# First layer of a top-1 expert network in arms of 256 and 320 columns, and rank matmuls ordered behind transposes

## The chip, the cores and the metric

One core of one Trainium2 chip runs the kernel. The metric is the device time of one execution in microseconds; times before are the median of three runs. PE is TensorE, DVE is VectorE, ACT is ScalarE, POOL is GpSimd and SP is SyncE, which issues most transfers.

## The reference

Two steps. The first is a kind of attention between 512 tokens and 32 state rows in each of 8 batches and 8 heads (head size 64), in both directions. Its output has 544 rows for each batch and 512 columns (all heads side by side), 4352 rows in all. The second sends each row to one of 8 experts, the one with the largest logit, and runs that expert's two layers on it:

```python
scores = scale * x @ state.T          # per batch and head; softmax over state
xread = a @ state
scores2 = scale * state @ x.T         # softmax over tokens
sread = a2 @ x
x = concat([xread, sread])            # (4352, 512)
logits = x @ w_gate; e_idx = argmax(logits, axis=1)
for e in range(8):
    mask = e_idx == e
    h = maximum(x[mask] @ w1[e], 0.0)          # 512 -> 1024
    ye = h @ w2[e]                             # 1024 -> 512
    out[mask] = gate_w[mask, None] * eom[mask, e, None] * ye
```

Matrix products are held to float32 quality: a factor is split into a high and a low part, and a product takes three matmuls (high by high, high by low, low by high).

## The kernel before

**Attention stage.** Batches follow each other in a software pipeline; a scheduler sets the order of instructions on each engine from their dependences, so that the order of PE is not the order of the source. For each batch PE transposes x (`x_trans`, L325), transposes the softmax of the other direction (`e2_trans`, L419), computes scores (L337), transposes the row softmax (`a_trans`, L359) and the scores for the softmax over columns (`columns_softmax`, L401), reads states (`state_reads`, L431) and reads tokens (`token_reads`, L380 to L382). After four batches the state rows get their logits (`state_out`, L444). When a group of batches has its logits, `route` (L221) finds each token's expert (the one-hot `ohb`), its rank among its expert's tokens, by matmuls with a triangle and with ones (L243 to L247), and its place in a table, by one matmul for each tile of 128 tokens into `tid_ps` (L300). PSUM has three double buffers `psb` for this stage and one buffer `pss`, which ranks and state reads share.

**Routing tables.** From the counts of each expert DVE works out tiles of 128 tokens, and from those units: two tiles a unit, an odd last tile joins its expert's last unit as a third, and an expert with a single tile has a unit of one (L507 to L581). `route_i` holds for each unit its size, whether it begins an expert, and which expert's weights to load next. Engines read these into registers and branch on them.

**Expert stage.** Written in order by hand (`manual_schedule`). For each unit `first` (L641) computes the first layer for all of the unit's tokens at once, 8 blocks of 12 matmuls, in an arm with 384 columns for three tiles and one with 256 columns otherwise; ACT and DVE turn each block into `hhi` and `hlo`. Then `second` (L666) runs 24 matmuls of 512 columns for one tile. Tile 0 is always run, tile 1 if the size is at least 2, tile 2 if it is 3. The other side of each of these branches is `nothing` (L660), one tiny matmul and a copy. Between them PE transposes the next unit's tokens (`x_transposed`, L611), two tiles and a third one if that unit has it. POOL gathers the tokens of the unit after next and scatters results by index. Where a unit begins an expert, ACT and DVE split the new weights into `whi` and `wlo`. First-layer results use four PSUM buffers `p1`, second-layer results two buffers `po`.

Of the kernel before, what the change touches and what calls it, by code (L numbers as in the profile page):

```python
# [9 lines left out]
F32 = mybir.dt.float32  # L10
# [4 lines left out]
ALU = mybir.AluOpType  # L15
# [6 lines left out]
def attention_then_top1_experts(ctx: ExitStack, tc: tile.TileContext, x, state, w_gate, w_og, w1, w2, out):  # L22
# [9 lines left out]
    W = 3  # L32
    NU = (NT - E + 1) // 2 + E
    NX = NU + NT // 2
# [6 lines left out]
    NQ = NT * E  # L41
    SURE = (NT - E) // 2

# [39 lines left out]
    unit_f = const.tile([1, NU], F32, name="unit_f")  # L83
    nc.gpsimd.tensor_copy(unit_f, un_i)

    def after(inst, before):
# [32 lines left out]
    with ExitStack() as actx:  # L119
# [101 lines left out]
        def route(lgs, nch, tile0, write):  # L221
# [67 lines left out]
            for c0 in range(0, nch, 3):  # L289
# [105 lines left out]
        def columns_softmax(b):  # L395
# [28 lines left out]
        def state_reads(b):  # L424

            xb, e2T = xbs[b], st["e2T", b]
            sr = pss.tile([P, 512], F32, name="pss", tag="pss")
            srv = sr.rearrange("p (h k n) -> p h k n", h=H, k=2)
            for h in range(H):
                for cc in range(2):  # L430
                    nc.tensor.matmul(srv[:, h], lhsT=xb[:, h, 2 * cc : 2 * cc + 2, :].rearrange("p c d -> p (c d)"),  # L431
                                     rhs=e2T[:, 2 * cc : 2 * cc + 2, NS * h : NS * h + NS], start=(cc == 0), stop=(cc == 1))
# [98 lines left out]
        r1 = slice(0, 1)  # L531
        nc.vector.scalar_tensor_tensor(ODD[r1], in0=LONE[r1], scalar=-2.0, in1=ODD[r1], op0=ALU.mult, op1=ALU.add)
        nc.vector.tensor_scalar(LAST[r1], SUM[r1], 1.0, None, op0=ALU.subtract)
# [57 lines left out]
    KH = DF // P  # L591
    NTOKU = W * P

    xg_all = [[bp1.tile([P, ROWW], F32, name=f"xg{u}{i}") for i in range(W)] for u in range(3)]
    xT_all = [[bp1.tile([P, KX, NTOKU], F32R, name=f"x{n}{u}") for n in ("hi", "lo")] for u in range(2)]
    hhi = bp1.tile([P, KH, NTOKU], F32R, name="hhi")
    hlo = bp1.tile([P, KH, NTOKU], F32R, name="hlo")
    rest_of = bp1.tile([P, 8], F32, name="rest_of")
# [12 lines left out]
    def x_transposed(u, i):  # L611
# [5 lines left out]
        for k in range(KX):  # L617
            nc.tensor.transpose(tp[:, k, :], xg_all[u % 3][i][:, P * k : P * k + P], ident)  # L618
        c = slice(P * i, P * i + P)
        nc.scalar.copy(hi[:, :, c], tp)  # L620
        nc.vector.tensor_sub(lo[:, :, c], tp, hi[:, :, c].bitcast(F32))  # L621

# [18 lines left out]
    def first(u, n, chg):  # L641

        hi, lo = xT_all[u % 2]
        for fb in range(KH):
# [7 lines left out]
            if fb in (0, 3):  # L652
                upper(2 if fb == 0 else 3, chg)
            nc.scalar.activation(hhi[:, fb, :n], p1[:, :n], AF.Relu)  # L654
            nc.vector.scalar_tensor_tensor(hlo[:, fb, :n], in0=p1[:, :n], scalar=0.0, in1=hhi[:, fb, :n].bitcast(F32),  # L655
                                           op0=ALU.max, op1=ALU.subtract)
            if fb in (1, 4):
# [8 lines left out]
    def second(u, t, between=None):  # L666
        po = py.tile([P, DM], F32, name="po", tag="po")
        c = slice(P * t, P * t + P)
        for j in (2, 3):
# [6 lines left out]
            for k in range(4):  # L676
# [5 lines left out]
                                     in_=y, in_offset=None)  # L682

    def values(u):
        if u >= NU:
            return None
        size = nc.values_load(route_i[0:1, 0, u : u + 1], engines=[ET.PE, ET.Activation, ET.DVE, ET.Pool], min_val=0, max_val=3,
                              skip_runtime_bounds_check_because="2, with one more for an odd number's last tile, or one less for an only one")
        if u == 0:
# [7 lines left out]
    def unit(u):  # L697
        size, chg, nxt = val[u]
        with tc.If(size == 3) as odd:
            first(u, NTOKU, chg)  # L700
        with odd.Else():
            first(u, 2 * P, chg)
# [11 lines left out]
        if more:  # L714
            x_transposed(u + 1, 1)
            with tc.If(more[0] == 3) as three:  # L716
                x_transposed(u + 1, 2)
            with three.Else():
# [5 lines left out]
        with tc.If(size == 3) as three:  # L724
            second(u, 2)
        with three.Else():
            nothing(py, "po")
# [46 lines left out]
```

## Time and profile before

| what | value |
|---|---|
| median of three runs (lowest, highest) | 660.9 us (660.82, 661.13) |
| the profiled execution, its time | 661.41 us |
| its span, first to last instruction | 659.7 us |
| PE busy | 615.5 us (93%) |
| VectorE, ScalarE, GpSimd busy | 283.4, 245.3, 176.9 us |
| mean granted clock of TensorE | 0.968 |

[...] Busy shares are means over two stages with different limits: the attention stage up to about 188 us, and the expert stage after it. Starts are in microseconds from the first instruction; a matmul's shown duration includes its way through the array, so that the time between starts, not the duration, says how fast matmuls follow each other.

### The profile page before, as it was taken

The page shows a single profiled execution, that of the slowest core. Times are in us where ns is not written, and L with a number is a line of the kernel's source. Part 1 is how long each engine was busy: PE and PEld are TensorE (multiplying, and loading weights), DVE is VectorE, ACT ScalarE, POOL GpSimd, SP SyncE. Part 2 cuts the span into 40 slices and gives each one's busy share as a digit, 9 for nine tenths or more (in the row PEclk, how much of TensorE's full clock was granted, in tenths as well). Part 3 has the DMA queues.
Part 4 walks back from the last instruction along what each step waited for, and adds up shares of the span by engine and source line. Part 5 has one row for each costly group of instructions (what it writes and reads, how often), then busy time and mean ns, then how long its engine had stood idle before and what let it go on. Part 6 is the DMA issues. An engine that isn't in the chain of part 4 may idle for free. (4 is left out here: it accounts for less than half of the span.)

```text
span 659.7 us, 11415 instructions
## 1 busy us (share of the span) xinstructions
PE 615.5 (93%) x3941; PEld 552.3 (84%) x3941; DVE 283.4 (43%) x622; ACT 245.3 (37%) x411; POOL 176.9 (27%) x254
## 2 busy tenths in 40 slices
PE   7899898998689999999999999999999999999990
PEld 5898797897468998998989989899898998988980
DVE  5547858979863211221235243144132514463210
ACT  3566536556042222222334244244233324472210
POOL 8135505531042221121122203123112220322210
PEclk8999979999779999999999999999999999999996
DMA  8534432322265220220145225326315523475210
GB/s 224 212 128 131 141 119 80 129 69 98 53 229 194 68 82 19 67 83 33 51 161 194 82 83 173 125 80 233 117 52 173 182 82 105 154 249 188 67 35 19
DMA packets 46289, 78.57 MB, mean 119 GB/s; under 512 B 11056, under 2 KB 19248, under 8 KB 46192
## 3 DMA queue, kind: packets, MB, share of 16 engines
q1 hardware_dynamic: 38592, 52.00, 23.9%
q0 software_dynamic: 7600, 25.38, 11.4%
q8 instruction: 49, 0.80, 0.5%
q14 instruction: 48, 0.39, 0.2%
HBM read 101.98 MB, written 19.42 MB: 184 GB/s over the span
## 5 line engine op out<-in xcount | busy, mean ns | idle before, releaser
L655 DVE SCALAR_TENSOR_TENSOR hlo<-p,hhi 128x256 fp32r<-128x256 f32 (+1 forms) x136 | 62.0, 462 | 224.8 <-ACT hhi L654 212.0
L648 PE MATMUL p<-xhi,whi 128*128 128x256 f32 (+1 forms) x544 | 151.0, 300 | 0.9 <-ACT rest_of L664 0.5
L649 PE MATMUL p<-xhi,wlo 128*128 128x256 f32 (+1 forms) x544 | 149.8, 298 | 0.0
L681 POOL DMA_INDIRECT out_dram<-y,idx x38 | 39.4, 1038 | 316.0 <-ACT y L680 228.0
L674 PE MATMUL po<-whi,hhi 128*128 128x512 f32 x304 | 122.6, 403 | 0.0
L675 PE MATMUL po<-wlo,hhi 128*128 128x512 f32 x304 | 120.1, 395 | 0.0
L654 ACT ACTIVATE hhi<-p 128x256 fp32r<-128x256 f32 (+1 forms) x136 | 56.2, 415 | 135.7 <-PE p L651 132.8
L648 PEld LDWEIGHTS p<-xhi,whi 128*128 128x128 f32 x544 | 103.4, 190 | 2.1 <-ACT rest_of L664 1.2
L649 PEld LDWEIGHTS p<-xhi,wlo 128*128 128x128 f32 x544 | 103.3, 190 | 0.3 <-issue 0.2
L651 PE MATMUL p<-xlo,whi 128*128 128x256 f32 (+1 forms) x544 | 95.8, 298 | 0.0
L678 PE MATMUL po<-whi,hlo 128*128 128x512 f32 x304 | 83.2, 395 | 0.0
L607 POOL DMA_INDIRECT xg<-xa,idx x57 | 68.4, 1200 | 49.5 <-issue 16.2
L651 PEld LDWEIGHTS p<-xlo,whi 128*128 128x128 f32 x544 | 81.1, 190 | 0.0
L680 ACT ACTIVATE y<-po,xg 128x512 f32<-128x512 f32 x38 | 26.1, 688 | 132.5 <-issue 49.1
L678 PEld LDWEIGHTS po<-whi,hlo 128*128 128x128 f32 x304 | 57.0, 187 | 14.0
L675 PEld LDWEIGHTS po<-wlo,hhi 128*128 128x128 f32 x304 | 57.2, 188 | 11.6
L674 PEld LDWEIGHTS po<-whi,hhi 128*128 128x128 f32 x304 | 57.1, 188 | 11.5
L635 DVE TENSOR_TENSOR wlo<-stage,whi 128x2048 fp32r<-128x2048 f32 x24 | 54.4, 2286 | 11.6 <-ACT whi L628 11.6
L621 DVE TENSOR_TENSOR xlo<-pxT,xhi 128x512 fp32r<-128x512 f32 x39 | 25.9, 687 | 62.4 <-ACT xhi L620 62.4
L628 ACT CAST whi<-stage 128x2048 fp32r<-128x2048 f32 x24 | 45.1, 1902 | 3.9 <-DVE hlo L655 1.7
L620 ACT CAST xhi<-pxT 128x512 fp32r<-128x512 f32 x39 | 22.2, 583 | 30.7 <-PE pxT L618 30.7
L337 PE MATMUL psb<-sT,xT 128*128 128x64 f32 x256 | 32.7, 289 | 0.2 <-ACT xT L327 0.2
(189 smaller groups left out, 728.2 us busy)
## 6 DMA issues: line engine op xcount, KB each, us to landing
stage<-in_moe_w_dram SPq DMA_DIRECT2D x74, 1024.0 KB
xb<-in_x_dram SPq DMA_DIRECT2D x7, 1024.0 KB
xa<-xm SPq DMA_DIRECT2D x7, 1024.0 KB
xb<-in_x_dram SPq DMA_DIRECT2D x2, 512.0 KB
xa<-xm SPq DMA_DIRECT2D x4, 256.0 KB
xg<-xa,idx POOLq DMA_INDIRECT x57, 3.6
out_dram<-y,idx POOLq DMA_INDIRECT x38, 3.1
sraw<-in_state_dram SPq DMA_DIRECT2D x2, 256.0 KB
```

Source lines behind the costliest of these rows:

```text
L607: g = nc.gpsimd.indirect_dma_start(out=xg_all[u % 3][i], out_offset=None, in_=xa[:, :], in_offset=bass.IndirectOffsetOnAxis(ap=ix, axis=0))
L628: nc.scalar.copy(whi[i], stage[i])
L635: nc.vector.tensor_sub(wlo[i], stage[i], whi[i].bitcast(F32))
L648: nc.tensor.matmul(p1[:, :n], lhsT=whi[i][:, k, c], rhs=hi[:, k, :n], start=(k == 0), stop=False)
L649: nc.tensor.matmul(p1[:, :n], lhsT=wlo[i][:, k, c], rhs=hi[:, k, :n], start=False, stop=False)
L651: nc.tensor.matmul(p1[:, :n], lhsT=whi[i][:, k, c], rhs=lo[:, k, :n], start=False, stop=(k == KX - 1))
L654: nc.scalar.activation(hhi[:, fb, :n], p1[:, :n], AF.Relu)
L655: nc.vector.scalar_tensor_tensor(hlo[:, fb, :n], in0=p1[:, :n], scalar=0.0, in1=hhi[:, fb, :n].bitcast(F32), op0=ALU.max, op1=ALU.subtract)
L674: nc.tensor.matmul(po, lhsT=hhi[:, f, c], rhs=whi[j][:, k, :], start=(f == 0), stop=False)
L675: nc.tensor.matmul(po, lhsT=hhi[:, f, c], rhs=wlo[j][:, k, :], start=False, stop=False)
L678: nc.tensor.matmul(po, lhsT=hlo[:, f, c], rhs=whi[j][:, k, :], start=False, stop=(f == KH - 1))
L681: nc.gpsimd.indirect_dma_start(out=out[:, :], out_offset=bass.IndirectOffsetOnAxis(ap=idx[:, W * u + t : W * u + t + 1], axis=0), in_=y, i ...
```

## The change

Three things are changed. The third tile joins a unit only if it holds at most 64 tokens; the first layer then has 256 + 64 = 320 columns, and the third tile's 64 tokens lie with their high and low parts side by side in one stationary operand of 128 (`hfew`), so that its second layer (`second_few`) takes 16 matmuls and the two halves of the result are added afterwards. An odd tile with more tokens gets a unit of its own of size 1. Sizes are now 1, 2 and 4, the tables hold 24 units instead of 21, and 14 units instead of 13 run without asking whether they exist. In the attention stage an order without a wait is asked for: a group's first rank matmul and its matmuls into `tid_ps` stand on PE behind the last column transposes or state reads that were written before them, except near the end of the stage.

```diff
-    NU = (NT - E + 1) // 2 + E
+    NU = NT // 2 + E - 1
-    SURE = (NT - E) // 2
+    HP = P // 2
+    FEW = 2 * P + HP
+    SURE = -(-NTOK // FEW)
...
+    def behind(inst, before):
+        tc.add_manual_dep(inst.ins, before.ins.name, mybir.DependencyInfo(mybir.DependencyClass.NoSync, mybir.DependencyReason.DATA), reason="order")
...
-            nc.tensor.matmul(rkv, lhsT=tri, rhs=ohb, start=True, stop=False)
+            m = nc.tensor.matmul(rkv, lhsT=tri, rhs=ohb, start=True, stop=False)
+            if len(done) < NT - 5:
+                behind(m, st["pe"])
...
                     done.append(nc.tensor.matmul(tid_ps, lhsT=pa, rhs=rb, start=(len(done) == 0), stop=(len(done) == NT - 1)))
+                    if len(done) < NT - 9:
+                        behind(done[-1], st["pe"])
...
-                    nc.tensor.transpose(tp[:, g, P * c : P * c + P], s_v[:, c, g, :], ident)
+                    st["pe"] = nc.tensor.transpose(tp[:, g, P * c : P * c + P], s_v[:, c, g, :], ident)
...
+            st["pe"] = m
...
-        nc.vector.tensor_scalar(LONE, TILES, 1.0, None, op0=ALU.is_equal)
         units = HALVES
-        odd0 = nc.vector.scalar_tensor_tensor(ODD, in0=HALVES, scalar=-2.0, in1=TILES, op0=ALU.mult, op1=ALU.add)
-        nc.vector.tensor_add(units, HALVES, LONE)
+        nc.vector.scalar_tensor_tensor(ODD, in0=HALVES, scalar=-2.0, in1=TILES, op0=ALU.mult, op1=ALU.add)
+        nc.vector.scalar_tensor_tensor(LAST, in0=TILES, scalar=-float(P), in1=cps[:, :E], op0=ALU.mult, op1=ALU.add)
+        nc.vector.tensor_scalar(LONE, TILES, 1.0, None, op0=ALU.is_gt)
+        nc.vector.scalar_tensor_tensor(LONE, in0=LAST, scalar=-float(HP), in1=LONE, op0=ALU.is_le, op1=ALU.mult)
+        nc.vector.tensor_tensor(LONE, LONE, ODD, op=ALU.mult)
+        nc.vector.tensor_add(units, HALVES, ODD)
+        nc.vector.tensor_sub(units, units, LONE)
...
+        n = P if i < 2 else HP
+        c = slice(P * i, P * i + n)
+        nc.scalar.copy(hi[:, :, c], tp[:, :, :n])
+        nc.vector.tensor_sub(lo[:, :, c], tp[:, :, :n], hi[:, :, c].bitcast(F32))
...
+            parts = [(hhi[:, fb], hlo[:, fb], 0, n)]
+            if n == FEW:
+                parts = [(hhi[:, fb], hlo[:, fb], 0, 2 * P), (hfew[:, fb, :HP], hfew[:, fb, HP:], 2 * P, FEW)]
+            for th, _, c0, c1 in parts:
+                nc.scalar.activation(th[:, : c1 - c0], p1[:, c0:c1], AF.Relu)
+            for th, tl, c0, c1 in parts:
+                nc.vector.scalar_tensor_tensor(tl[:, : c1 - c0], in0=p1[:, c0:c1], scalar=0.0, in1=th[:, : c1 - c0].bitcast(F32),
+                                               op0=ALU.max, op1=ALU.subtract)
...
+    def second_few(u):
+        po = py.tile([P, DM], F32, name="po", tag="po")
+        for f in range(KH):
+            nc.tensor.matmul(po, lhsT=hfew[:, f, :], rhs=whi[2 + f // 4][:, f % 4, :], start=(f == 0), stop=False)
+            nc.tensor.matmul(po, lhsT=hfew[:, f, :], rhs=wlo[2 + f // 4][:, f % 4, :], start=False, stop=(f == KH - 1))
+        y2 = bp.tile([HP, DM], F32, name="y2", tag="y2", bufs=1)
+        nc.scalar.copy(y2, po[HP:])
+        y = bp.tile([P, DM], F32, name="y", tag="y", bufs=3)
+        nc.vector.tensor_add(y2, y2, po[:HP])
+        nc.scalar.activation(y[:HP], y2, AF.Copy, scale=xg_all[u % 3][2][:HP, DM : DM + 1])
...
-        with tc.If(size == 3) as odd:
-            first(u, NTOKU, chg)
+        with tc.If(size == 4) as few:
+            first(u, FEW, chg)
```

The place of the ranks on PE, in the fourth batch of the attention stage, where the ranks are those of the second group (`ohb_859`). Each L337 or L347 row is scores, L359 or L369 the transposes of the row softmax, L401 or L411 the column transposes, L431 or L441 state reads, L380 or L390 token reads. Before:

```order
L419 MATMUL psb<-ident,e_783 128x128 x8
L337 MATMUL psb<-sT,xT 128x2x32 x4
L243 LDWEIGHTS tri
L243 MATMUL pss<-ohb_859,tri 128x64
...
L247 MATMUL pss<-run_bf,ones 128x64
L337 MATMUL psb<-sT,xT 128x2x32 x12
L359 MATMUL psb<-ident,a_sb 128x128 x8
L431 MATMUL pss<-e2T,xb 128x64 x2
L401 MATMUL psb<-ident,s_sb 128x128 x8
L431 MATMUL pss<-e2T,xb 128x64 x14
```

After:

```order
L429 MATMUL psb<-ident,e_783 128x128 x8
L347 MATMUL psb<-sT,xT 128x2x32 x16
L369 MATMUL psb<-ident,a_sb 128x128 x8
L411 MATMUL psb<-ident,s_sb 128x128 x8
L249 LDWEIGHTS tri
L249 MATMUL pss<-ohb_859,tri 128x64
...
L255 MATMUL pss<-run_bf,ones 128x64
L390 MATMUL psb<-sbd_181,aThi 128x272
...
L441 MATMUL pss<-e2T,xb 128x64 x16
L455 MATMUL psb<-idw,srT 128x80 x8
```

The ranks moved from the middle of the scores to behind both groups of transposes, and the state reads from ahead of the token reads to behind them, directly ahead of the state logits.

The third tile's end on ACT, in one unit of the expert stage: the result of tile 1, the branch, and the result of tile 2. Before:

```order
L680 ACTIVATE y<-po,xg_2167 128x512
L720 UNCONDITIONAL_BRANCH
L664 COPY rest_of<-po 128x8
L720 UNCONDITIONAL_BRANCH
L724 COMPARE_AND_BRANCH
L680 ACTIVATE y<-po,xg_2168 128x512
```

After:

```order
L701 ACTIVATE y<-po,xg_2171 128x512
L755 UNCONDITIONAL_BRANCH
L685 COPY rest_of<-po 128x8
L755 UNCONDITIONAL_BRANCH
L759 COMPARE_AND_BRANCH
L712 COPY y_2636<-po 64x512
L715 ACTIVATE y<-y_2636,xg_2172 64x512
```

One activation of 128 rows became a copy of 64 rows out of PSUM and an activation of 64 rows, with an addition on DVE between the two.

## Rows read from the trace of the kernel before

**Rows 1.** Busy time by stretch: us, each engine's busy (instructions), granted clock, DMA share, GB/s

```profile
76.24:81.34 5.10, 2.25 (x25) 2.07 (x26) 3.71 (x10) 3.89 (x6) 4.79 (x9) 1.00 0.54 184
81.34:91.58 10.24, 10.24 (x56) 10.24 (x52) 6.41 (x24) 2.30 (x3) 1.20 (x5) 0.50 0.40 121
154.00:160.60 6.60, 3.90 (x35) 3.26 (x34) 6.37 (x24) 3.76 (x5) 0.34 (x1) 1.00 0.42 159
...
187.10:193.95 6.85, 6.30 (x28) 5.90 (x29) 3.36 (x12) 2.98 (x4) 1.89 (x2) 0.50 0.94 321
188.76:644.10 455.34, 454.33 (x2725) 408.42 (x2725) 146.19 (x210) 151.46 (x264) 103.61 (x91) 0.99 0.35 119
```

**Rows 2.** PE in order of time, expert stage: start, us, instruction, [idle before, releaser]

```profile
261.91 0.36 PE L648 MATMUL p<-xhi,whi 128*128 128x256 f32 x1
...
273.30 0.39 PE L674 MATMUL po<-whi,hhi 128*128 128x512 f32 x1
...
285.51 0.36 PE L648 MATMUL p<-xhi,whi 128*128 128x256 f32 x1
...
309.44 0.42 PE L648 MATMUL p<-xhi,whi 128*128 128x384 f32 x1
...
326.17 0.39 PE L674 MATMUL po<-whi,hhi 128*128 128x512 f32 x1
...
332.65 0.47 PE L674 MATMUL po<-whi,hhi 128*128 128x512 f32 x1
...
343.94 0.28 PE L648 MATMUL p<-xhi,whi 128*128 128x256 f32 x1
...
566.37 0.28 PE L648 MATMUL p<-xhi,whi 128*128 128x256 f32 x1
...
585.42 0.39 PE L648 MATMUL p<-xhi,whi 128*128 128x256 f32 x1 [0.51 <-ACT rest_of L664]
```

**Rows 3.** Groups by shape, PE: count, busy us, mean ns, idle before

```profile
L648 PE MATMUL p<-xhi,whi 128*128 128x384 f32 x160 | 54.2, 338 | 0.0
```

**Rows 4.** PE in order of time, fourth batch of the attention stage

```profile
77.45 1.09 PE L419 MATMUL psb<-ident,e 128*128 128x128 f32 x8 [1.21 <-ACT xm L383]
78.38 1.09 PE L337 MATMUL psb<-sT,xT 128*128 128x64 f32 x8
81.11 0.19 PE L243 MATMUL pss<-ohb,tri 128*128 128x64 bf16 x1 [1.64 <-DVE ohb L235]
...
81.34 5.36 PE L337 MATMUL psb<-sT,xT 128*128 128x64 f32 x24
...
98.97 1.91 PE L444 MATMUL psb<-idw,srT 128*128 128x80 f32 x16
100.72 1.91 PE L325 MATMUL psb<-ident,xb 128*128 128x128 f32 x16
```

**Rows 5.** Groups, ACT and DVE: 512-element results out of PSUM

```profile
L620 ACT CAST xhi<-pxT 128x512 fp32r<-128x512 f32 x39 | 22.2, 583 | 30.7 <-PE pxT L618 30.7
...
L621 DVE TENSOR_TENSOR xlo<-pxT,xhi 128x512 fp32r<-128x512 f32 x39 | 25.9, 687 | 62.4 <-ACT xhi L620 62.4
```

**Rows 6.** PE in order of time, a later batch of the attention stage

```profile
123.04 3.68 PE L337 MATMUL psb<-sT,xT 128*128 128x64 f32 x32
126.56 1.05 PE L359 MATMUL psb<-ident,a_sb 128*128 128x128 f32 x8
...
134.30 3.79 PE L431 MATMUL pss<-e2T,xb 128*128 128x64 f32 x32
137.92 1.92 PE L325 MATMUL psb<-ident,xb 128*128 128x128 f32 x16
```

**Rows 7.** PE in order of time, the second state logits

```profile
168.00 1.20 PE L444 MATMUL psb<-idw,srT 128*128 128x80 f32 x9 [0.73 <-DVE srT L435]
```

**Rows 8.** DVE and PE in order of time, where the expert stage begins

```profile
184.99 0.17 DVE L581 CAST route_i<-uf 1x42 int32<-1x42 f32 x1
...
188.76 0.58 PE L648 MATMUL p<-xhi,whi 128*128 128x256 f32 x1 [0.31 <-issue]
```

More of the change, by code (lines that the diff above doesn't have):

```diff
@@ L430, in state_reads @@
                 for cc in range(2):
-                    nc.tensor.matmul(srv[:, h], lhsT=xb[:, h, 2 * cc : 2 * cc + 2, :].rearrange("p c d -> p (c d)"),
+                    m = nc.tensor.matmul(srv[:, h], lhsT=xb[:, h, 2 * cc : 2 * cc + 2, :].rearrange("p c d -> p (c d)"),
                                      rhs=e2T[:, 2 * cc : 2 * cc + 2, NS * h : NS * h + NS], start=(cc == 0), stop=(cc == 1))
+            st["pe"] = m
             t2, bb = b // 4, b % 4
@@ L531, in attention_then_top1_experts @@
         r1 = slice(0, 1)
-        nc.vector.scalar_tensor_tensor(ODD[r1], in0=LONE[r1], scalar=-2.0, in1=ODD[r1], op0=ALU.mult, op1=ALU.add)
+        nc.vector.scalar_tensor_tensor(ODD[r1], in0=LONE[r1], scalar=3.0, in1=ODD[r1], op0=ALU.mult, op1=ALU.subtract)
         nc.vector.tensor_scalar(LAST[r1], SUM[r1], 1.0, None, op0=ALU.subtract)
@@ L591, in attention_then_top1_experts @@
     KH = DF // P
-    NTOKU = W * P
     xg_all = [[bp1.tile([P, ROWW], F32, name=f"xg{u}{i}") for i in range(W)] for u in range(3)]
-    xT_all = [[bp1.tile([P, KX, NTOKU], F32R, name=f"x{n}{u}") for n in ("hi", "lo")] for u in range(2)]
-    hhi = bp1.tile([P, KH, NTOKU], F32R, name="hhi")
-    hlo = bp1.tile([P, KH, NTOKU], F32R, name="hlo")
+    xT_all = [[bp1.tile([P, KX, FEW], F32R, name=f"x{n}{u}") for n in ("hi", "lo")] for u in range(2)]
+    hhi = bp1.tile([P, KH, 2 * P], F32R, name="hhi")
+    hlo = bp1.tile([P, KH, 2 * P], F32R, name="hlo")
+    hfew = bp1.tile([P, KH, P], F32R, name="hfew")
     rest_of = bp1.tile([P, 8], F32, name="rest_of")
@@ L618, in x_transposed @@
             nc.tensor.transpose(tp[:, k, :], xg_all[u % 3][i][:, P * k : P * k + P], ident)
-        c = slice(P * i, P * i + P)
-        nc.scalar.copy(hi[:, :, c], tp)
-        nc.vector.tensor_sub(lo[:, :, c], tp, hi[:, :, c].bitcast(F32))
+        n = P if i < 2 else HP
+        c = slice(P * i, P * i + n)
+        nc.scalar.copy(hi[:, :, c], tp[:, :, :n])
+        nc.vector.tensor_sub(lo[:, :, c], tp[:, :, :n], hi[:, :, c].bitcast(F32))
     def upper(i, chg):
@@ L653, in first @@
                 upper(2 if fb == 0 else 3, chg)
-            nc.scalar.activation(hhi[:, fb, :n], p1[:, :n], AF.Relu)
-            nc.vector.scalar_tensor_tensor(hlo[:, fb, :n], in0=p1[:, :n], scalar=0.0, in1=hhi[:, fb, :n].bitcast(F32),
-                                           op0=ALU.max, op1=ALU.subtract)
+            parts = [(hhi[:, fb], hlo[:, fb], 0, n)]
[6 more added lines that the diff above has]
+                                               op0=ALU.max, op1=ALU.subtract)
             if fb in (1, 4):
@@ L682, in second @@
                                      in_=y, in_offset=None)
+    def second_few(u):
[8 more added lines that the diff above has]
+        nc.scalar.activation(y[:HP], y2, AF.Copy, scale=xg_all[u % 3][2][:HP, DM : DM + 1])
+        nc.gpsimd.indirect_dma_start(out=out[:, :], out_offset=bass.IndirectOffsetOnAxis(ap=idx[:HP, W * u + 2 : W * u + 3], axis=0),
+                                     in_=y[:HP], in_offset=None)
     def values(u):
@@ L686, in values @@
             return None
-        size = nc.values_load(route_i[0:1, 0, u : u + 1], engines=[ET.PE, ET.Activation, ET.DVE, ET.Pool], min_val=0, max_val=3,
-                              skip_runtime_bounds_check_because="2, with one more for an odd number's last tile, or one less for an only one")
+        size = nc.values_load(route_i[0:1, 0, u : u + 1], engines=[ET.PE, ET.Activation, ET.DVE, ET.Pool], min_val=0, max_val=4,
+                              skip_runtime_bounds_check_because="2, or 1 or 4 at the end of an odd number")
         if u == 0:
@@ L698, in unit @@
         size, chg, nxt = val[u]
-        with tc.If(size == 3) as odd:
-            first(u, NTOKU, chg)
-        with odd.Else():
+        with tc.If(size == 4) as few:
+            first(u, FEW, chg)
+        with few.Else():
             first(u, 2 * P, chg)
@@ L715, in unit @@
             x_transposed(u + 1, 1)
-            with tc.If(more[0] == 3) as three:
+            with tc.If(more[0] == 4) as few:
                 x_transposed(u + 1, 2)
-            with three.Else():
+            with few.Else():
                 nothing(ph, "p1")
@@ L723, in unit @@
             nothing(py, "po")
-        with tc.If(size == 3) as three:
-            second(u, 2)
-        with three.Else():
+        with tc.If(size == 4) as few:
+            second_few(u)
+        with few.Else():
             nothing(py, "po")
```

## Prediction

> **What bounds the kernel now.** I read the page's busy times first, then the busy times by stretch, then the order of time on TensorE (PE). The expert stage runs from 188.76 us to the end of the last matmul at 644.10 us, and PE is busy for 454.33 of these 455.34 us at a granted clock of 0.99 [rows 1]. So a change to this stage is worth what it adds to or takes from PE's own work, and nothing that other engines do counts unless it starves PE. The stage is a chain of 17 units that repeat to within a few hundredths. A unit of two tiles takes 285.51 - 261.91 = 23.60 us, of which the first layer is 273.30 - 261.91 = 11.39. A unit of three tiles takes 343.94 - 309.44 = 34.50, its first layer 326.17 - 309.44 = 16.73, and its last two second layers (48 matmuls) 343.94 - 332.65 = 11.29, that is 0.235 each. A unit of one tile takes 585.42 - 566.37 = 19.05, with a wait of 0.51 at its end [rows 2]. The 384-column shape occurs 160 times, 32 to a unit: five units have three tiles [rows 3].
>
> In the attention stage PE also waits. The worst place is around 81 us. [...]
>
> **The change, part by part.** I sum against the profiled execution's own 661.41 us (span 659.7). The median of the three runs, 660.9, is 0.5 below it.
>
> *Which arms are taken.* Routing the reference's inputs gives the eight experts 1568, 632, 512, 541, 513, 40, 0 and 546 tokens. That makes 13, 5, 4, 5, 5, 1, 0 and 5 tiles and fits the trace (17 units, five of three). The last tiles of the experts with an odd number above one hold 32, 120, 29, 1 and 34 tokens. So four experts take the new arm of 320 columns, and the second expert (120) gets a unit of its own: 18 units.
>
> *Four few arms.* First layer: 96 matmuls of 320 columns, halfway between 11.39 and 16.73 = 14.06, so -2.67. (If time went by columns from either shape it would be 13.94 or 14.24.) Third tile's second layer: 16 matmuls instead of 24, 8 x 0.235 = -1.88. Together -4.55 a unit, -18.2 in all.
>
> *The second expert.* One unit of three (34.50) becomes one of two and one of one (23.60 + 19.05): +8.15. More overheads of a unit, such as its skipped arms and the wait of 0.51, are inside the 19.05.
>
> *End of the kernel.* The last unit is a few arm. After its last matmul ScalarE now copies 64x512 out of PSUM and VectorE adds, before the activation that stood there already. By the nearest rows of 512 elements these are 0.583 and 0.687 [rows 5]: +1.27. Elsewhere the same two steps hide under the next unit's first layer; ScalarE's queue then starts the next expert's weight cast 1.3 us later, with four PSUM buffers of 11.39/8 = 1.42 us each as cover.
>
> *Ranks.* In the fourth batch the rank matmuls now stand behind the score matmuls and both groups of transposes. The wait of 1.64 goes, since ohb is there at 81.11, before PE comes to it. What is next late is taken from the undisturbed later batch: from its scores at 123.04 to its row transposes at 126.56 is 3.52, from there to its state reads at 134.30 is 7.74 (transposes of both kinds, ranks, token reads and the waits among them), and 3.62 to 137.92 [rows 6]. State reads also move behind token reads here, as in that batch. From 78.38: 78.38 + 3.52 + 7.74 + 3.62 = 93.26. Then the state logits must wait for VectorE's two copies of srT, which the state reads no longer precede by far. The one row of that wait shows 0.73, with other matmuls between that hid part of it [rows 7]; here nothing stands between, so I take 1.3, an estimate of not quite twice as much, and keep 0.73 as the other end. With 100.72 - 98.97 = 1.75 for the logits, the next batch starts at 96.3, where it stood at 100.72 [rows 4]: -4.4. This holds only if the clock does not fall. The waits of 1.21 and then about 0.35 and 1.15 are spread over some ten microseconds, and a denser stretch (154.00 to 160.60, PE busy 3.90 of 6.60) kept the clock at 1.00 [rows 1], so I take it that it stays. If it falls after all, half of 10.24 comes back: -4.4 + 5.1 = +0.7, the bad end, a loss. In the other batches ranks and lookups change places with transposes just ahead of a wait for aTlo that PE reaches anyway; I put them at 0, within 0.4 either way each. No load stands in the way of an earlier start: PE's waits there name ScalarE, VectorE and GpSimd, none a DMA.
>
> *Routing tables.* VectorE gets four more small operations, and tables for 24 units instead of 21, before the table's last write at 184.99. PE comes to read it at the end of its transposes, for a first matmul at 188.76 [rows 8]; three microseconds of cover, so 0, and about 0.5 if the cover were gone.
>
> Sum: -18.2 + 8.15 + 1.27 - 4.4 = -13.2, so 648.2 for the profiled execution and **647.7** by the median.
>
> [...] At the single unit's end a branch was followed by 0.51 us without a matmul, while the whole stage, with a skipped arm or two at each of 17 units, lost only 1.0 us [rows 1, 2]. [...]
>
> **The rivals.** (1) As above: 647.7, with its own range 646.0 to 649.5 from the ends of the few arm's first layer (0.5), of the end (0.4), of srT (0.6) and of the other batches. (2) The clock falls once in the attention stage all the same. For it: the 1.21 before 77.45 stays, and two new waits follow. Against it: the denser stretch at full clock. 660.9 - 18.2 + 8.15 + 1.27 + 0.7 = 652.8. (3) With the attention stage shifted, the stretch at 0.50 before and in the first unit (187.10 to 193.95, PE busy 6.30) [rows 1] shrinks or goes: up to 3.1 less, 644.6. Nothing in the diff aims at it. (4) Skipped arms stall: four branches in the new unit at the 0.51 seen once, 649.7. (5) Slower. The few arm's longer ending on ScalarE and VectorE delays the next expert's casts, PE runs out of PSUM buffers, and the clock falls. That can happen behind three of the four few arms, those followed by another expert (the last has none). Each would cost half of 10.24 and some 0.5 of stall, 5.6, so 647.7 + 16.8 = 664.5. It decides from the point where PE idles as it did before 81.34, 2.85 of 5.10 us. Against it: 1.3 us of delay under 5.7 us of buffers. (6) It doesn't do what it says: were one of the four last tiles over 64 tokens on the chip, its expert would need 23.60 + 19.05 instead of 29.95, +12.7, so 660.4. Against it: the largest is 34.
>
> **How the numbers follow.** Chances: (1) 0.60, (2) 0.22, (3) 0.07, (4) 0.05, (5) 0.03, (6) 0.03. The likeliest gives the time, 647.7. The range takes in cases 1, 4 and 2 (652.8, with 0.7 for its own terms) and the near part of 3: 645.5 to 653.5. A measurement of this kernel can tell about 0.2% (1.3 us) from no change. Faster by more: cases 1 to 4, 0.94. Within 0.2%: case 6, 0.03. Slower: case 5, 0.03.
>
> **What would show it.** Few arms: 128 matmuls of 320 columns for each of the first layer's three lines, a first layer near 14.06 us, and 29.95 from such a unit's start to the next. Second expert: three units of 23.6, 23.6 and 19.05. End: some 1.3 us more from last matmul to the end of the span than 15.6. Ranks: no wait for ohb near 81 us, a granted clock of 1.00 from 76 to 100 us, and the fifth batch's transposes near 96. I would be wrong if the clock row still has its dip there, if PE idles more than a few tenths at any change of expert, or if the expert stage is not about 445.3 us long (455.34 - 10.05).

## The result and the profile after

The changed kernel takes 652.46 us (median of 4 runs, 651.65 to 654.97) against 660.86 for the kernel before: a ratio of 0.9882, 95% interval 0.9853 to 0.9911. Timed again on another chip it took 651.4 against 659.85, ratio 0.9862 (0.9847 to 0.9877). A ratio, here and below, is formed from the single runs and is not the quotient of the two medians. The time lies in the predicted range, but not at the likeliest case of 647.7: it is that of the second rival, 652.8, in which the clock falls once in the attention stage all the same, and it is in the range because the range was drawn to take that rival in.

The profiled execution takes 652.26 us with a span of 650.24, where it was 661.41 and 659.70. The 9.15 us between them are -10.21 in the expert stage, +0.02 up to its first matmul (188.78, was 188.76), +0.73 from the last matmul to the end, and +0.31 outside the span. So all of the gain is in the expert stage, and the attention stage gave nothing where 4.4 was expected. One thing in this comparison isn't of the change: this trace is 0.87 late at its first scores already, before anything that was reordered. Before and after:

```profile
14.93 1.10 PE L337 MATMUL psb<-sT,xT 128*128 128x64 f32 x8 [0.23 <-ACT xT L327]
15.80 1.11 PE L347 MATMUL psb<-sT,xT 128*128 128x64 f32 x8
```

The low stretch of the clock near the start lasts 6.83 us here, from 7.96, and 3.41 in the trace before, from 9.62. In both traces it ends before the first scores, that is before anything that was reordered. Counted from the first scores, the attention stage is 0.85 shorter.

Busy time by stretch of the changed kernel (us, then PE, weight loads, VectorE, ScalarE, GpSimd with their instructions, the granted clock as a share of TensorE's full speed, DMA share, GB/s), beside [rows 1]:

```profile
81.34:96.21 14.87, 11.45 (x97) 10.32 (x96) 12.61 (x31) 7.75 (x14) 7.21 (x19) 1.00 0.49 165
96.70:103.53 6.83, 6.83 (x35) 6.83 (x34) 5.18 (x16) 2.22 (x4) 3.65 (x6) 0.50 0.56 152
188.78:633.91 445.13, 443.43 (x2798) 398.02 (x2798) 149.54 (x254) 155.81 (x313) 103.51 (x94) 1.00 0.37 124
```

The stretch at 0.50 that stood at 81.34 to 91.58, behind the waits of 1.21 and 1.64 [rows 4], is gone from there, and one of 6.83 us stands at 96.70 to 103.53. The expert stage is 445.13 us long, PE busy for all but 1.70 of it.

PE in order of time in the expert stage, beside [rows 2]: the starts of a two-tile unit, of a few arm's first layer and its second layers, of the unit after it, and of the second expert's single tile:

```profile
284.75 0.37 PE L664 MATMUL p<-xhi,whi 128*128 128x256 f32 x1
...
308.68 0.39 PE L664 MATMUL p<-xhi,whi 128*128 128x320 f32 x1
...
322.84 0.39 PE L695 MATMUL po<-whi,hhi 128*128 128x512 f32 x1
...
338.75 0.28 PE L664 MATMUL p<-xhi,whi 128*128 128x256 f32 x1
...
385.85 0.36 PE L664 MATMUL p<-xhi,whi 128*128 128x256 f32 x1
...
404.32 0.17 PE L684 MATMUL po<-ones 128*128 128x8 bf16 x1 [0.42 <-ACT y L701]
404.83 0.39 PE L664 MATMUL p<-xhi,whi 128*128 128x256 f32 x1 [0.34 <-ACT rest_of L685]
```

A few arm's first layer takes 322.84 - 308.68 = 14.16, the whole unit 338.75 - 308.68 = 30.07, the single tile 404.83 - 385.85 = 18.98. The groups by shape, beside [rows 3], show 4 x 32 instructions of 320 columns in each of the three lines:

```profile
L664 PE MATMUL p<-xhi,whi 128*128 128x320 f32 x128 | 38.3, 310 | 0.0
```

PE in the fourth batch of the attention stage and at the start of the fifth, beside [rows 4]:

```profile
78.29 1.09 PE L429 MATMUL psb<-ident,e 128*128 128x128 f32 x8 [1.38 <-ACT xm L393]
79.22 3.79 PE L347 MATMUL psb<-sT,xT 128*128 128x64 f32 x32
...
85.05 0.19 PE L249 MATMUL pss<-ohb,tri 128*128 128x64 bf16 x1
...
86.70 0.39 PE L392 MATMUL psb<-sbd,aTlo 128*128 128x272 f32 x1 [0.92 <-DVE aTlo L373]
...
89.63 0.39 PE L390 MATMUL psb<-sbd,aThi 128*128 128x272 f32 x1 [0.43 <-ACT xm L393]
...
90.58 3.79 PE L441 MATMUL pss<-e2T,xb 128*128 128x64 f32 x32
96.21 3.22 PE L455 MATMUL psb<-idw,srT 128*128 128x80 f32 x16 [1.84 <-DVE srT L446]
99.22 3.62 PE L335 MATMUL psb<-ident,xb 128*128 128x128 f32 x16
```

The rank matmul at 85.05 waits for nothing now, and all 32 score matmuls run through. But the state logits wait 1.84 for srT, and right behind that, at 96.70, the clock falls to 0.50: the logits take 3.01 to the next start instead of 1.75, and the fifth batch's transposes 3.62 instead of 1.91. What VectorE did in that time, and GpSimd beside it, in order of time:

```profile
93.28 2.01 DVE L304 TENSOR_SCALAR rb<-iota_q,sm,vid 128x272 fp32r<-128x272 f32 x1
95.21 0.85 DVE L446 COPY srT<-pss 64x256 f32<-64x256 f32 x2
...
96.89 1.26 DVE L290 TENSOR_SCALAR sm<-sm 128x8 f32<-128x8 f32 x1
```

```profile
93.22 1.91 POOL L361 TENSOR_TENSOR a_sb<-a_sb,st 128x1024 f32<-128x1024 f32 x1
...
96.85 2.50 POOL L501 TENSOR_TENSOR wlo<-stage,whi 128x512 fp32r<-128x512 f32 x2
```

The copies of srT stand in VectorE's queue behind rb, and rb takes 2.01 us, where others of its shape take 0.41. It ends 0.16 us after GpSimd's product a_sb ends at 95.13. Likewise a 128x8 operation takes 1.26 beside one piece of GpSimd's wlo.

The end of the kernel, ScalarE and VectorE behind the last matmul at 633.91:

```profile
633.99 0.58 ACT L712 COPY y<-po 64x512 f32<-64x512 f32 x1 [3.03 <-PE po L710]
635.31 0.72 ACT L715 ACTIVATE y<-y,xg 64x512 f32<-64x512 f32 x1 [0.75 <-DVE y L714]
```

```profile
634.60 0.68 DVE L714 TENSOR_TENSOR y<-y,po 64x512 f32<-64x512 f32 x1 [8.58 <-ACT y L712]
```

### The profile page after: what moved, and what is told of

Its sections match the earlier page's. It is cut to its first block, busy times and chain, and to the rows that moved or that the text cites. A ratio compares the mean times of both kernels' runs of the same rounds, so it can differ in the third digit from the quotient of the medians.

```text
span 650.2 us, 11847 instructions
## 1 busy us (share of the span) xinstructions
PE 603.5 (93%) x4014; PEld 541.6 (83%) x4014; DVE 289.6 (45%) x671; ACT 250.3 (38%) x461; POOL 176.3 (27%) x257
## 5 line engine op out<-in xcount | busy, mean ns | idle before, releaser
L676 DVE SCALAR_TENSOR_TENSOR hlo<-p,hhi 128x256 fp32r<-128x256 f32 x144 | 59.6, 423 | 183.5 <-ACT hhi L674 113.9
L695 PE MATMUL po<-whi,hhi 128*128 128x512 f32 x272 | 110.2, 405 | 0.0
L696 PE MATMUL po<-wlo,hhi 128*128 128x512 f32 x272 | 107.4, 395 | 0.0
L674 ACT ACTIVATE hhi<-p 128x256 fp32r<-128x256 f32 x144 | 54.6, 384 | 123.6 <-PE p L667 83.2
L699 PE MATMUL po<-whi,hlo 128*128 128x512 f32 x272 | 74.4, 395 | 0.0
L699 PEld LDWEIGHTS po<-whi,hlo 128*128 128x128 f32 x272 | 51.0, 187 | 12.5
L696 PEld LDWEIGHTS po<-wlo,hhi 128*128 128x128 f32 x272 | 51.2, 188 | 10.0
L637 DVE TENSOR_TENSOR xlo<-pxT,xhi 128x512 fp32r<-128x512 f32 (+1 forms) x40 | 25.6, 661 | 68.4 <-ACT xhi L636 68.4
L636 ACT CAST xhi<-pxT 128x512 fp32r<-128x512 f32 (+1 forms) x40 | 22.0, 561 | 33.5 <-PE pxT L633 33.5
L441 PE MATMUL pss<-e2T,xb 128*128 128x64 f32 x256 | 30.1, 274 | 0.4 <-DVE t L267 0.4
```

What stands on the lines that cost most here:

```text
L674: nc.scalar.activation(th[:, : c1 - c0], p1[:, c0:c1], AF.Relu)
L676: nc.vector.scalar_tensor_tensor(tl[:, : c1 - c0], in0=p1[:, c0:c1], scalar=0.0, in1=th[:, : c1 - c0].bitcast(F32), op0=ALU.max, op1=ALU.s ...
L695: nc.tensor.matmul(po, lhsT=hhi[:, f, c], rhs=whi[j][:, k, :], start=(f == 0), stop=False)
L696: nc.tensor.matmul(po, lhsT=hhi[:, f, c], rhs=wlo[j][:, k, :], start=False, stop=False)
L699: nc.tensor.matmul(po, lhsT=hlo[:, f, c], rhs=whi[j][:, k, :], start=False, stop=(f == KH - 1))
```

## Experiments

Theory A: the whole gain is PE's own work in the expert stage; the ordering of the ranks took one wait away and met the next. Theory B: the ordering is worth its 4 us, and another part of the change ate them. Theory E came up on the way: VectorE, held up beside GpSimd, owes PE its results at much the same times wherever PE's matmuls stand.

**The arms alone.** The two calls of `behind` are left out:

```diff
-            if len(done) < NT - 5:
-                behind(m, st["pe"])
...
-                    if len(done) < NT - 9:
-                        behind(done[-1], st["pe"])
```

> The changed kernel without its ordering: the ranks and the tile lookups may stand where they stood before, and all else of the change stays. [...] Theory B (the ordering is worth the 4 us of the prediction and something else of the change, such as the longer routing tables or the later start of the fourth batch, ate them): first expert matmul 3 to 4 us later than in the changed kernel, time near 656 us.

Measured: 649.94 us, ratio 0.9833 (0.9801 to 0.9866); first expert matmul at 187.85, expert stage 444.99. The wait for ohb is back, and a low stretch of 6.83 us follows from 82.69. PE in order of time:

```profile
81.88 0.19 PE L249 MATMUL pss<-ohb,tri 128*128 128x64 bf16 x1 [1.64 <-DVE ohb L241]
```

The first expert matmul is not later than in the changed kernel, but 0.9 earlier, and the time is lower if anything: 649.94 us against the changed kernel's 652.46, where theory A has the two the same. Theory B falls.

**The ordering alone**, in the kernel before: the function `behind`, its two calls and the two assignments of `st["pe"]` from the change, and nothing else.

> The kernel before with only the ordering of ranks and lookups behind the transposes and state reads; units, arms and tables are those of before. Theory A: the wait at 81 us goes, the wait for srT near 96 us grows to some 1.8 us, the clock falls there instead, first expert matmul within 0.5 us of 188.8, time 660.5 to 661.3 us, the same as before. Theory B: first expert matmul near 185, time near 656.5 us.

Measured: 659.7 us against 661.26, ratio 0.9974 (0.9955 to 0.9994); first expert matmul 186.90, expert stage 455.50. Both theories missed: 1.86 us are gained in the attention stage, neither 0 nor 4. The wait for srT is the one of the changed kernel, to the hundredth, but the clock fell behind it for 3.41 us instead of 6.83:

```profile
93.97 2.42 PE L452 MATMUL psb<-idw,srT 128*128 128x80 f32 x16 [1.84 <-DVE srT L443]
```

The other difference lies 20 us earlier. In the changed kernel PE waits 1.38 us at 78.29; in this run it doesn't. What goes with it is there in the traces, some 4 us earlier. VectorE (a 128x2 operation), GpSimd (a_sb) and PE in order of time, first of the changed kernel (the wait of 1.38 is shown above):

```profile
73.98 1.93 DVE L417 TENSOR_SCALAR st<-st 128x2 f32<-128x2 f32 x1 [0.15 <-ACT e L416]
```

```profile
73.98 1.92 POOL L361 TENSOR_TENSOR a_sb<-a_sb,st 128x1024 f32<-128x1024 f32 x1 [8.41 <-ACT e L416]
```

and then of a run in which VectorE came through, the ordering with srT on ScalarE (below):

```profile
73.41 0.17 DVE L417 TENSOR_SCALAR st<-st 128x2 f32<-128x2 f32 x1
```

```profile
73.40 1.95 POOL L361 TENSOR_TENSOR a_sb<-a_sb,st 128x1024 f32<-128x1024 f32 x1 [8.33 <-ACT e L416]
```

The two operations start within 0.02 us of each other. In the first trace VectorE's 0.17 us become 1.93, ScalarE's next step is late, and PE waits 1.4; in the second VectorE comes through. The recorded starts don't tell the two apart: GpSimd stands level or 0.01 ahead in both. In the ten traces with the ordering it went against VectorE in four (both of the changed kernel among them) and for it in six. In the four without the ordering GpSimd is ahead by 0.2 us each time, VectorE always takes 1.74 to 1.77, and PE waits 1.2. So a loss that all four without the ordering have there is one that four of the ten with it have, which no step of the prediction had in it. Only the changed kernel was traced twice, and it fell the same way both times, so whether this is chance or set by each kernel isn't shown. Nor is it shown by a run of its own that it accounts for all of the 0.26%.

**The changed kernel again**, unaltered, on the chip of later runs.

> The changed kernel unaltered, timed beside the others and with a second trace. Of the runs so far, the ordering alone had its first expert matmul at 186.90 us (before 188.76) and the arms alone had it at 187.85 (changed kernel 188.78). Theory A (the ordering gives nothing that can be told from the spread of the clock's low stretches): ratio to before 0.983 to 0.988, the same as the arms alone (0.9833). Theory B (the ordering is worth some 1.5 to 2 us, as in the run of the ordering alone, and the first trace fell badly): ratio near 0.981, first expert matmul near 187.

Measured: 651.4 us, ratio 0.9862 (0.9847 to 0.9877), first expert matmul 189.84, and once more the wait of 1.4 near 78, the wait of 1.83 for srT and a low stretch of 6.83 us. The five traces with the ordering and an otherwise unchanged attention stage have their first expert matmul at 186.90 to 189.84, mean 188.3; the three without it at 187.85 to 188.94, mean 188.5. Counted from each trace's first scores the means are 172.7 with the ordering and 173.0 without. The ordering gives nothing that stands out from the spread. Theory A holds for the sum; in the traces a wait of 1.64 went and one of 1.84 came.

**srT's copies on ScalarE**, for the fourth batch, so that they don't queue behind rb:

```diff
-                nc.vector.tensor_copy(srT[D * k : D * k + D, :, NS * bb : NS * bb + NS], srv[D * k : D * k + D, :, k, :])
+                copy = nc.scalar.copy if b == 3 else nc.vector.tensor_copy
+                copy(srT[D * k : D * k + D, :, NS * bb : NS * bb + NS], srv[D * k : D * k + D, :, k, :])
```

> The changed kernel with the fourth batch's two copies of srT on ScalarE instead of VectorE, where they stood behind a copy (rb) that lay 2.01 us beside a GpSimd operation. Theory A: PE's wait for srT near 96 us shrinks from 1.84 us to under 1.0. If that keeps the clock at its upper level from 96 to 104 us, the fifth batch's transposes start near 97 and its row transposes near 100 us instead of 103.95, so that 2.5 to 4 us are gained there; the first expert matmul then stands near 186 and the time near 649.5 us. If the clock falls all the same, under 1 us is gained: 651.5 to 652.5. Theory C (the attention stage behind 104 us is bound by VectorE and GpSimd's chain, or by the gather's landing, not by PE): the clock stays up and the fifth batch starts 2.5 to 4 us earlier, but by the state reads of the sixth batch at 117.7 us most of it is gone, first expert matmul at 188.3 to 188.8, time 652 us.

Measured: 650.33 us, ratio 0.9842 (0.981 to 0.9875); first expert matmul 189.22. PE, VectorE and ScalarE in order of time:

```profile
93.10 2.01 PE L456 MATMUL psb<-idw,srT 128*128 128x80 f32 x16 [0.83 <-ACT srT L447]
94.94 1.91 PE L335 MATMUL psb<-ident,xb 128*128 128x128 f32 x16
99.10 1.97 PE L429 MATMUL psb<-ident,e 128*128 128x128 f32 x8 [2.24 <-ACT xs L460]
```

```profile
96.10 1.25 DVE L290 TENSOR_SCALAR sm<-sm 128x8 f32<-128x8 f32 x1
...
98.08 0.28 DVE L458 TENSOR_REDUCE lgt<-psb 128x16 f32<-128x128 f32 x1
```

```profile
98.40 0.65 ACT L460 COPY xs<-psb 128x256 f32<-128x256 f32 x2 [5.35 <-DVE lgt L458]
```

The wait for srT shrank as expected and the clock stayed up through it. Then a wait of 2.24 us appeared where there had been none: PE needs the buffer that ScalarE's xs gives back, ScalarE had been idle 5.35 us for VectorE's lgt, and VectorE came to that only at 98.08, behind a 128x8 operation of 1.25 and a 128x128 one of 1.38 beside GpSimd's weight casts. The clock fell at the end of that wait, at 99.04, for 10.24 us, and in this trace the gain was lost. This is Theory C's result by a way that it didn't name; theory E is drawn from it.

**Filler matmuls in the wait**: 24 matmuls of 128 columns between the state reads and the state logits, unused results.

```diff
+                    if b == 3 and h == 0:
+                        for _ in range(24):
+                            f = nc.tensor.matmul(px[:, 0, 384:], lhsT=ones, rhs=ones, start=True, stop=True)
+                            behind(f, st["pe"])
+                            st["pe"] = f
...
```

> The changed kernel with 24 matmuls of 128 columns, whose results go unused, in TensorE's wait for srT near 96 us. Theory D (the wait itself costs little; the fall of the clock behind it costs the 3 us): the clock stays at its upper level through 96 to 104 us, the score matmuls of the fifth batch start near 101 instead of 103.95, the first expert matmul near 186.5, time 2 to 3 us below the changed kernel. Theory E (VectorE's queue is the bound there, and any time that TensorE saves is waited for at the next thing VectorE or ScalarE owes it): the clock stays up at 96 but a later wait of 1 to 2 us appears before the score matmuls, and the clock falls behind that, or the gain is under 1 us by the state reads near 117.7; time the same as the changed kernel within 0.2%.

Measured: 651.98 us, ratio 0.9873 (0.9857 to 0.989). The granted clock stayed at 1.00 from 65 to 153 us. PE in order of time:

```profile
93.34 1.50 PE L457 MATMUL psb<-ones 128*128 128x128 bf16 x24
95.24 2.01 PE L460 MATMUL psb<-idw,srT 128*128 128x80 f32 x16 [0.40 <-DVE srT L446]
...
100.68 1.09 PE L429 MATMUL psb<-ident,e 128*128 128x128 f32 x8 [1.69 <-ACT xs L466]
...
193.43 0.28 PE L672 MATMUL p<-xhi,wlo 128*128 128x256 f32 x1 [2.25 <-issue]
```

Both theories are half right. The clock was kept and the sixth batch's state reads start at 115.43 instead of 117.66; but 1.69 of waiting came up at the next thing owed, and the first expert matmul is only 1.3 earlier (187.51). The profiled run then lost 2.25 us in the first unit, in an idle time that the profile gives no releaser for. The time is that of the changed kernel: in these runs, holding the clock up through this stretch was not enough.

**GpSimd's casts later.** On top of srT on ScalarE, the casts of expert weights that stood in the third batch's turn move two batches on, out of VectorE's way at 93 to 98 us:

```diff
-            if 1 <= b <= 4:
-                i = (b - 1) // 2
-                for k in (0, 1) if b % 2 else (2, 3):
+            if b in (1, 2, 4, 5):
+                i = b // 4
+                for k in (0, 1) if b in (1, 4) else (2, 3):
```

> The run with srT's copies on ScalarE, and GpSimd's weight casts of the third batch moved two batches on, so that VectorE's work between 93 and 98 us is not beside them (a 128x8 operation took 1.25 us there, a 128x128 one 1.38, against 0.2 to 0.3 and 0.5 elsewhere). Theory E: VectorE reaches the reduction of the state logits near 96 instead of 98.08, TensorE's wait before the transposes of e2 shrinks from 2.24 to under 0.7 us, the clock stays at its upper level to 106 us, first expert matmul near 185.5, time 3 to 4 us below the changed kernel. Rival: the casts meet another piece of VectorE's work two batches on, or the clock falls elsewhere in the attention stage, and the time is that of the run with srT on ScalarE, 650.3.

Measured: 646.56 us, ratio 0.9819 (0.9792 to 0.9846), against 0.9862 for the changed kernel in the same set of runs; first expert matmul at 181.93, 7.3 earlier than with the copies alone. VectorE and PE in order of time:

```profile
94.27 0.19 DVE L290 TENSOR_SCALAR sm<-sm 128x8 f32<-128x8 f32 x1
...
95.19 0.28 DVE L458 TENSOR_REDUCE lgt<-psb 128x16 f32<-128x128 f32 x1
```

```profile
92.83 2.01 PE L456 MATMUL psb<-idw,srT 128*128 128x80 f32 x16 [0.83 <-ACT srT L447]
...
96.42 1.04 PE L429 MATMUL psb<-ident,e 128*128 128x128 f32 x8
```

The same 128x8 operation takes 0.19 instead of 1.25, lgt comes at 95.19 instead of 98.08, the wait of 2.24 is gone, and so is the fall of the clock. Busy time by stretch, first the changed kernel, then this one:

```profile
65.00:150.00 85.00, 76.62 (x621) 72.41 (x621) 66.74 (x157) 46.07 (x72) 34.10 (x67) 0.96 0.32 105
```

```profile
65.00:150.00 85.00, 77.45 (x647) 72.52 (x646) 72.57 (x170) 51.03 (x84) 35.70 (x65) 1.00 0.32 105
```

Theory E holds here, with more gained than it expected in this trace. But the trace is that of the fastest of six runs, and not every run gains: four took 645.6 to 647.2, two 650.5 and 650.8 at a lower mean clock (0.966 and 0.964 against 0.969 to 0.974). By all runs the step from the copies alone is from 0.9842 to 0.9819, with intervals that overlap.

**The casts and copies without the ordering**: the two edits above on the arms alone.

> The arms alone (no ordering of ranks and lookups) with the same two moves on ScalarE and GpSimd. Theory E (VectorE beside GpSimd held the ordering's gain back; the ordering removes the wait for ohb near 81 us and the two moves remove what came in its place): here the wait of 1.6 us for ohb is still there, the clock still falls near 82 us, first expert matmul near 187.5, time the same as the arms alone, 649.5 to 650 us. Rival (the two moves alone bring the gain, with or without the ordering): first expert matmul near 182 to 184, time near 646.5.

Measured: 649.66 us, ratio 0.9833 (0.9806 to 0.9861), the same as the arms alone; first expert matmul at 186.82.

```profile
81.06 0.21 PE L249 MATMUL pss<-ohb,tri 128*128 128x64 bf16 x1 [1.64 <-DVE ohb L241]
```

The wait is there, and the clock fell for 10.24 us from 80.97. The two edits alone don't gain what they gain with the ordering.

**The casts alone**, on the changed kernel, srT's copies left on VectorE.

> The changed kernel with GpSimd's casts of the third batch two batches on and nothing else. The wait of 1.84 us for srT should stay, since the GpSimd operation beside rb is another one (the product that ends the softmax). Theory E: the clock falls behind that wait as in the changed kernel, VectorE is free earlier behind it (the reduction of the state logits follows the logits at once), time 650 to 651.5 us. Rival (the casts alone had held VectorE up): the wait for srT shrinks to under 1 us, time near 646.5.

Measured: 651.48 us, ratio 0.9851 (0.982 to 0.9881); PE waits 1.83 for srT at 95.09, and the clock falls within that wait, at 93.96, for 6.83 us. So in the traces all three are needed: the ordering against the wait for ohb, the copies on ScalarE against the wait for srT, the casts' move against the wait for xs. Each of the three pairs leaves one wait, and in its one trace the clock falls at it. The times say less: the interval of all three together (0.9792 to 0.9846) overlaps those of the two pairs timed here (0.9806 to 0.9861 and 0.982 to 0.9881) and that of the arms alone (0.9801 to 0.9866).

**Fewer columns: 296.** Third tiles of at most 40 tokens; the largest is 34.

```diff
-    HP = P // 2
+    HP = 40
+    LP = P // 2
...
-        nc.vector.scalar_tensor_tensor(LONE, in0=LAST, scalar=-float(HP), in1=LONE, op0=ALU.is_le, op1=ALU.mult)
+        nc.vector.scalar_tensor_tensor(LONE, in0=LAST, scalar=-float(P - HP), in1=LONE, op0=ALU.is_le, op1=ALU.mult)
...
-                parts = [(hhi[:, fb], hlo[:, fb], 0, 2 * P), (hfew[:, fb, :HP], hfew[:, fb, HP:], 2 * P, FEW)]
+                parts = [(hhi[:, fb], hlo[:, fb], 0, 2 * P), (hfew[:, fb, :HP], hfew[:, fb, LP : LP + HP], 2 * P, FEW)]
...
```

> The changed kernel with arms of 296 columns instead of 320 (third tiles of at most 40 tokens instead of 64); the same four experts take them (last tiles of 32, 29, 1 and 34 tokens). If the first layer's time goes by columns between the measured 11.39 us (256) and 14.16 us (320), 296 columns take 11.39 + 40/64 x 2.77 = 13.12 us, 1.04 less in each of four units: expert stage 441.0 us, time near 648.3 us. The rival is that a matmul of such width has a floor or a step (its weight load, or a row of 320 and 296 columns costing the same): first layer 14.1 us, time 652.5 us as in the changed kernel.

Measured: 648.84 us, ratio 0.9807 (0.9776 to 0.9839). A few arm's first layer takes 13.21 (13.12 expected), 0.95 less than at 320, 3.8 in four units. The expert stage shrank by only 2.3, to 442.83: the rest is the first unit, where the clock is low at the start in either trace (25.79 instead of 25.18), the first layers behind the single tiles (0.45 in all) and some 0.05 in each of the nine other two-tile units. Without the ordering the same arms gave

> Arms of 296 columns and no ordering of ranks and lookups: the arms alone, with 0.95 us less in each of four first layers. Theory A: 3.8 us below the arms alone, ratio 0.9833 - 0.0057 = 0.9776 to before, within 0.3% of the run of 296 columns with the ordering (0.9807). Theory B: 2 us slower than with the ordering, ratio near 0.983.

649.07 us, ratio 0.9829 (0.9817 to 0.9842), expert stage 442.45. The ratio is the one that theory B named, but the intervals of the two runs overlap, and their first expert matmuls, at 188.94 without the ordering and 188.15 with it, are closer than the two of the changed kernel; the pair decides nothing.

**Fewer still: 288.** `HP = 32`, so that the last expert's tile of 34 falls out.

> Arms of 288 columns, third tiles of at most 32 tokens: the last expert, whose last tile has 34, gets a unit of its own. By the rows so far a few arm of 288 columns has a first layer of 11.39 + 32/64 x 2.77 = 12.78 (1.38 less in each of three units, -4.1); the last expert's last two tiles take 23.6 and 19.0 instead of one few arm of 30.07, +12.5; the end is shorter by the 0.7 of the copy and the addition. Sum +7.7 against the changed kernel's 651.4 to 652.5: near 659.5 us, 19 units.

Measured: 659.07 us, ratio 0.9978 (0.9959 to 0.9998); 19 units, first layer of a few arm 12.83 (12.78 expected), expert stage 454.44. The price of one tile too large is as expected, and it is nearly all of the change's gain. The end was not shorter by 0.7 but longer by 0.7; that was not followed up.

**Both gains together**: arms of 296 columns, the ordering, srT on ScalarE and the casts later.

> Arms of 296 columns, ordering kept, srT's copies of the fourth batch on ScalarE and GpSimd's casts of the third batch two batches on: the two gains together. If they add: 646.56 (casts moved) less 4 x 0.95 = 642.8 us, with runs near 641.8 where the clock stays up through the attention stage and near 647 where it falls. If the shift of the attention stage meets the memory transfers of the first unit or the clock's fall at the stage's end differently, 644 to 646.

Measured: 644.71 us (642.42 to 648.94), ratio 0.9781 (0.9744 to 0.9818), below the changed kernel's interval on either chip; against the same arms with none of the three steps the two intervals just meet (0.9817 to 0.9842). The median is that of the second case expected, 644 to 646, and the single runs lie on both sides of it. First expert matmul 182.14, expert stage 442.37, again in the trace of the fastest of six runs. Its median is the lowest of all.

## Why the prediction was right and wrong

*Few arms, -18.2.* Right. The first layer is 14.16 for 14.06, the unit 30.07 for 29.95: 0.1 saved too little in each of four units, -17.7 in all. Between 256 and 384 columns the time goes nearly by columns: a first layer's time over its 96 matmuls is 118.7 ns at 256, 133.6 at 288, 137.6 at 296, 147.5 at 320, and 174.3 at 384 in the trace before.

*Second expert, +8.15.* Right: 23.51 + 23.59 + 18.98 = 66.08 instead of 402.28 - 343.94 = 58.34 in the trace before, +7.74. The expert stage as a whole is 445.13 for 445.29, and that it is so close is in part luck: the two terms give -9.95, and the first unit, in which the clock starts low in either trace, took 25.18 instead of 25.94. In the second trace of the changed kernel it took 25.92, and the stage 445.78.

*End, +1.27.* Mis-sized: +0.73. The copy (0.58) and the addition (0.68) cost what [rows 5] said, and the activation starts 1.40 after the last matmul. But from the activation's end to the end of the span it is 14.2 us instead of 14.8. There are 64 rows to write instead of 128, but no run shows that this is why.

*Ranks, -4.4.* Wrong: 0, or -0.85 counted from the first scores. The working failed in the step "what is next late", and in two ways. First, srT: the estimate of 1.3 came from doubling a row of another place, not from what stands ahead of srT on VectorE. There stood rb, at 2.01 us instead of 0.41, and the wait was 1.84. Second, "I take it that it stays", of the clock. The waits of 0.92, 0.43 and 1.84 between 86.70 and 96.21 were followed by 6.83 us at a granted clock of 0.50; with 0.92, 0.43 and 0.83, in the run with srT's copies on ScalarE, it stayed at 1.00 until the later wait of 2.24. The denser stretch from which the prediction argued was no guide to this one. From 96.3 the fifth batch moved to 99.22: 0.84 because this run was that late at 79.22 already (0.87 at its first scores), 0.71 more from the state reads to the logits (the wait alone was 1.84 for 1.3), 1.26 for logits at a granted clock of 0.50, 0.1 in the rest. What was left against 100.72 was gone by the sixth batch's state reads, which start at 117.66 in both traces. A small misreading stands beside it: of PE's waits in the trace before, two do name a DMA, the gather of xg, 0.67 at 185.93 and 0.75 at 187.34.

*Routing tables, 0.* Nothing shows against it: the first expert matmul stands at 188.78 for 188.76, and the table's last write still ends 2.7 us ahead of it.

*Rivals.* (2) is what happened, for the reasons that it gave: new waits in place of the old, and one fall of the clock; it had 0.22 against the 0.60 of the case that failed. Its price was a little different, 6.83 us of low clock instead of 10.24. (3) no: the low stretch at the start of the first unit is 6.83 us as before. (4) no: a skipped arm's own matmul takes 0.03 to 0.04 us of PE's time, and the 0.42 and 0.34 behind the single tile name ScalarE, as the 0.51 of the trace before does [rows 2], so no trace bears out a stall of the skipped arms. (5) no: the stage's granted clock is 1.00, and PE waits nowhere behind a few arm. It does behind the two single tiles, 0.42 + 0.34 and 0.42 + 0.40; that is inside the price of 19.05, of which 18.98 and 18.95 were taken. (6) no: four few arms ran. The run of 288 columns shows that its price, one more unit, had the right size.

## What to carry to other kernels

When an order is changed so that PE no longer waits for one result, look up what the engine that owes it has in its queue when PE comes to the next result, and beside which other engine's work; here a wait that was only covered by the one before it came out at much the same size: 1.64 for ohb went and 1.84 for srT came, and with that one down to 0.83 there came 2.24 for xs. Three waits of 1.6 to 2.2 us stood in a row here, and in the traces of the pairs the clock fell at the one that was left; with fillers in one wait it stayed up, and the time was no shorter. Only the two kernels in which all three were gone brought the first expert matmul to 182, and their medians are 4.8 and 4.1 us below those of the same arms with the ordering alone; two of six runs of each still took 648 to 651. Work that PE does itself, in a stage where PE is busy for 443.43 of 445.13 us, came out here within 0.14 us a unit of its sum from the rows.

## What the runs showed of the hardware

Three of VectorE's operations took about as long as the GpSimd operation beside them, whatever their own size: 128x272 in 2.01 us instead of 0.41, 128x2 in 1.93 instead of 0.17, 128x8 in 1.26 instead of 0.19. All three are `tensor_scalar` operations, they end with the GpSimd operation or up to 0.2 us behind it, and the 128x8 one took 0.19 once GpSimd's casts had been moved. Why they take that long was not shown, nor what decides it when the starts of the two lie within 0.02 us.

The two traces of the changed kernel differ by one more low stretch of the clock, 3.41 us near 161, and their first expert matmul stands at 188.78 and 189.84. With that spread, with low stretches of 3.41 or 6.83 us near the start and near ties such as the one at 74 us, an edit to the attention stage that is worth 1 us can't be told from one trace.

In at least three traces PE stood idle for 1.12 to 2.25 us in the course of a first layer of the expert stage, with no releaser: the 2.25 at 193.43 in the run with fillers, and these in the runs of 288 columns and of both gains together:

```profile
580.39 0.39 PE L668 MATMUL p<-xlo,whi 128*128 128x256 f32 x1 [1.55 <-issue]
```

```profile
575.06 0.39 PE L669 MATMUL p<-xlo,whi 128*128 128x256 f32 x1 [1.12 <-issue]
```

What PE waited for there was not shown.
